# Sliding-window attention into a gated layer on one core: the first tile's first layer by halves of its weights, 96 tiny matmuls at the start, and some scores run twice

## The chip, the core and the metric

The kernel runs on one core of a Trainium2 chip. The metric is the device time of one execution in microseconds (us), as the median of several runs. Engines are written as in the profile: PE is TensorE's matmul, PEld its weight load, DVE is VectorE, ACT ScalarE, POOL GpSimd and SP SyncE.

## What is computed

Attention with a causal window of 64 positions over 8 batches, 8 heads, 576 positions and 64 values per head, then a gated layer on the 4608 rows that come out (512 wide, 1536 hidden):

```python
scores = scale * np.matmul(q, k.transpose(0, 1, 3, 2))
mask = (rel >= 0) & (rel < window)          # rel = query position - key position
attn = softmax(np.where(mask, scores, -1e9))
x = np.matmul(attn, v)                      # then heads side by side: (4608, 512)
gate = np.maximum(x @ w_gate, 0.0)
val = x @ w_val
out = (gate * val) @ w_out                  # float32
```

## The kernel before

The rows are cut into tiles: four of 384 rows (tiles 0 to 3) and six of 512. Attention is made in units of 192 rows, two for each of the first four tiles. A unit's scores are small matmuls in four row groups of 32 partitions (`st_block`, line 265), each block of 64 columns in two parts; `u_exp` (ACT) and `u_mask` (DVE) follow, `u_pv` multiplies with v (line 336), `u_recip`, `u_norm` and `u_turn` (DVE, and for half of unit 1 ACT in `u_norm_act`) divide and transpose the result into `xt`, the layer's input. For units 0 and 1 the mask is written into the score banks beforehand by matmuls of an identity with a bias tile (`bias_mm`, line 232, called by `u_bias`).

Tiles 0 and 1 use the plain layer, `hidden`: for a group of up to four blocks of 128 hidden columns it first runs the gate weights `wg` and then the value weights `wv` (line 589), each with four products that accumulate over the four 128-row chunks c of xt. ACT takes the gate result to SBUF (`relu`, line 572), DVE multiplies it with the value result out of PSUM into `g_sb` (`gate`, line 575). Results go to single PSUM banks 0 to 3 in turn (`one_bank`); units use banks 4 to 7 in pairs (`two_banks`). Tile 0's first group runs over two spans of 192 rows, unit 0's and then unit 1's; the other groups of tile 0 over all 384 rows. Tile 1 does its first 192 rows, then part of tile 0's output (`output`, line 1023), then its other rows. Tiles 2 and later use a scheme with seven products in place of eight (`fast_hidden`, line 634, and for the last six tiles also `SevenOut` and `SevenLast`, line 847), whose sums of weights DVE and POOL form on the way (`w_form`).

`w_load` brings four blocks of wg or wv by two transfers issued on POOL, one for chunks 0 and 1 and one for chunks 2 and 3. POOL also copies v rows (`v_spread`, line 215), loads q, k and v, and so its order of issue is written out by hand.

A planner (`Weaver`, `W`) writes the order in which instructions are emitted. It has a clock of its own, in which every matmul has a cost; `W.at(T, fn)` puts a piece of work in a heap for time T, and `W.advance` emits all that is due. `w_need` moves the clock to the time that `w_load` was told for the weights' landing. These times are no waits on the chip: they decide only the order on each engine. On the chip, engines wait for one another by semaphores on tiles and banks.

`keep_hot` and `heat` are matmuls on a cleared tile. The order of the products of each late tile is a list of names; for the last tile but one it is `SEVEN[-1]`, where P5a and P5b are two parts of product P5 and "v0", "v1" and "h1" are attention values and the beginning of the next tile's layer.

Of the kernel before, what the change touches and what calls it, by code (L numbers as in the profile page):

```python
# [47 lines left out]
def kernel(  # L48
# [20 lines left out]
    G = 4  # L69
# [84 lines left out]
    def w_load(wt, src, f0, f1, landed):  # L154

        if wt is not wo:
            ns = slice(128 * f0, 128 * f1)
            for a in range(2):
                nc.gpsimd.dma_start(wt[:, 2 * a:2 * a + 2, ns], src.rearrange("(a p e) n -> a p e n", a=2, e=2)[a, :, :, ns])  # L159
        if wt is wo:  # L160
            nc.gpsimd.dma_start(wo[:, f0:f1], src.rearrange("(c p) n -> p c n", p=128)[:, f0:f1])
        w_done.update(((wt.name, f), landed) for f in range(f0, f1))

    def w_need(wt, f):
        while (wt.name, f) not in w_done:
            W.pop()
        W.advance(w_done[wt.name, f])

# [51 lines left out]
        for g0, g1 in (((2, 3),), ((4, 5),), ((6, 9),))[uu]:  # L220
            rows(t[0:64, g0:g1:2], t[64:128, g0 - 1:g1 - 1:2])

    def heat(n, to, start=True):

        for _ in range(n):
            nc.tensor.matmul(to, zero[:, 0:128], zero[:, 0:to.shape[1]], start=start, stop=start, skip_group_check=not start)

    def keep_hot(to):
        nc.tensor.matmul(to, zero32[:, 0:128], zero32[:, 0:to.shape[1]], start=False, stop=False, skip_group_check=True)
# [31 lines left out]
    def st_block(to, g, hh, n, biased=False, later=False):  # L261

        b, w = divmod(n, NG)
        rows = slice(32 * g, 32 * g + 32)
        return [lambda dh=dh: nc.tensor.matmul(  # L265
            to, kTs[b % 2][rows, hh, 64 * w:64 * w + 128, dh], qTs[b % 2][rows, hh, 64 * w:64 * w + 64, dh],
            start=(dh == 0 and not biased and not later), stop=(dh == 1), skip_group_check=biased or later) for dh in range(2)]

    def run_rows(rows):

        for step in zip(*rows):
            for dh in range(2):
                for block in step:
                    block[dh]()
# [5 lines left out]
            bias_mm(units[u]["st"][c])  # L280
        units[u]["biased"] = True

    def u_st(u, hhs=(0, 1)):
        d = units.setdefault(u, {})
        if "st" not in d:
            st_tiles(u)
        run_rows([[st_block(d["st"][g][:, U * hh + 64 * w:U * hh + 64 * w + 64], g, hh, UB * u + w, "biased" in d)
                   for hh in hhs for w in range(UB)] for g in range(G)])
        return 0.29 * len(hhs)

    def p_of(u, h, w):
# [262 lines left out]
        while normed[0] < n:  # L554
            W.pop()

    def hidden(t, spans, f0=0, f1=NF, each=1):

        if t not in gs:
            gs[t] = g_sb_p.tile([128, NF, WT], FP16, name="g_sb"), {}  # L560
        g_sb, done = gs[t]
        xt = xt_tile(t)
        n = spans[0][1] - spans[0][0]

        w = 512 // n
        each = max(each, w)

        def part(tile):
            return tile[:, 0:w * n].rearrange("p (w n) -> p w n", w=w)

        def relu(r_sb, h1):
            nc.scalar.activation(part(r_sb), part(h1), ACT.Relu)  # L572

        def gate(f, c0, r_sb, h2):
            nc.vector.tensor_tensor(g_sb[:, f:f + w, c0:c0 + n], part(r_sb), part(h2), MUL)
            done.update(dict.fromkeys(range(f, f + w), c0 + n))

        for fb in range(f0, f1, each):
            r2s = [f_sb.tile([128, 2, WT], FP32, name="pr", bufs=4) for _ in range(2)]
            r_sbs = {}  # L580
            for i, wt in enumerate((wg, wv)):
                for c0, f in ((c0, f) for c0, _ in spans for f in range(fb, fb + each, w)):
                    h = one_bank()
                    part_written([h])
                    for b in range(w):
                        W.advance(W.clock)
                        w_need(wt, f + b)
                        for c in range(NC):
                            nc.tensor.matmul(h[:, b * n:b * n + n], wt[:, c, (f + b) * 128:(f + b) * 128 + 128],  # L589
                                             xt[:, c, c0:c0 + n], start=(c == 0), stop=(c == NC - 1))  # L590
                        W.clock += 4 * (n + 7) / 2400.0
                    if i == 0:
                        r_sb = r_sbs[c0, f] = r2s[len(r_sbs) // 2][:, len(r_sbs) % 2]
                        W.at(W.clock, lambda r_sb=r_sb, h=h: relu(r_sb, h))
                    else:
                        W.at(W.clock, lambda f=f, c0=c0, r_sb=r_sbs[c0, f], h=h: gate(f, c0, r_sb, h))

    def fast_hidden(t, seven=None):

# [467 lines left out]
    XAT = -0.3  # L1067
    SEVEN_LAST = (("P6", "P5", "P2", "P7", "oP1", "P3", "P4"), ("P6", "P5", "P2", "P7", "oP1", "P4", "P3"))
    SEVEN = {n: ("P2", "v0", "v1", "P6", "P5a", "P7", "s0", "P5b", "P4", "s1", "P3") for n in (-5, -4, -3, -2)}
    SEVEN[-1] = ("v0", "P2", "P6", "v1", "P5a", "P7", "P5b", "P4", "h1", "P3")  # L1070

    SEVEN[0] = ("P2", "P4", "P5", "P6", "P7", "P3")

    with tc.manual_schedule():
# [21 lines left out]
        k_zeros()  # L1096
        band_bias()

        first_round("k", (dve, act))
        u_bias(0)  # L1100
        u_bias(1)
# [21 lines left out]
        u_turn(0)  # L1123
        for hh in range(2):
            u_pv(1, (hh,), True)
        heat(1, units[1]["st"][3])
# [6 lines left out]
        w_load(*G3[1], 20.3)  # L1133
        w_load(*V3[1], 22.8)
        v_load(2)
        w_load(*G3[2], 27.0)
        w_load(*V3[2], 29.6)
        W.at(23.2, lambda: u_st(2))
        plan_exps(23.2, 2)
        plan_values(27.4, 2)  # L1140

        v_spread(2, pool)
        for name in "kq":
            for hh in range(2):
                qk_load(1, name, hh)
# [3 lines left out]
        for u in (4, 5):  # L1149
            v_load(u)  # L1150
        for i, (name, hh) in enumerate((n, hh) for n in "kq" for hh in range(2)):
            W.at(31.6 + 1.4 * i, lambda name=name, hh=hh: qk_trans(1, name, hh))
        for hh, T in enumerate((36.6, 38.8)):
            W.at(T, lambda hh=hh: u_st(3, (hh,)))
            for i in range(G):
                W.at(T + 0.4 + 0.22 * i, lambda hh=hh, i=i: u_exp(3, i, (hh,)))
                W.at(T + 0.8 + 0.22 * i, lambda hh=hh, i=i: u_mask(3, i, (hh,)))
            W.at(T + 3.5 - 0.7 * hh, lambda hh=hh: u_pv(3, (hh,)))
            W.at(T + 4.0 - 0.7 * hh, lambda hh=hh: u_recip(3, (hh,)))
            W.at(T + 4.1 - 0.7 * hh, lambda hh=hh: u_norm(3, hh))  # L1160
            W.at(T + 4.6 - 0.7 * hh, lambda hh=hh: u_turn(3, (hh,)))
        W.at(37.4, lambda: v_spread(3, pool))
        W.at(40.6, lambda: behind_masks(3))

        def pair(t, TA, TB, P):
            for u, T in ((2 * t, TA), (2 * t + 1, TB)):
# [10 lines left out]
            W.at(T + 1.9, lambda: u_turn(u))  # L1177
            return took

        plan_batch(2, (36.5, 36.6, 42.5, 42.6), (52.0, 53.6, 56.9, 57.1))  # L1180
        plan_batch(3, 58.0, None)
        W.at(58.0, lambda: v_load(8))
        for u in (6, 7):
# [1 line left out]
            W.at(58.0, lambda u=u: v_spread(u))  # L1185
        for u in (4, 5):
            W.at(45.6, lambda u=u: v_spread(u))
        pair(2, 46.6, 50.0, 54.0)
        W.at(52.7, lambda: behind_masks(5))
        pair(3, 62.6, 65.3, None)  # L1190
        W.at(68.0, lambda: behind_masks(7))
# [28 lines left out]
        def ahead(t):  # L1220
            T = W.clock
            long = widths[t] == WT
            ends = T + (32.7 if long else 22.5)
            if t + 2 <= LAST:
                qk_turns(t + 2, T, LATE if t - 1 in FAST_OUT else (0.1, 1.4, 8.0, 14.2) if long else (0.1, 1.4, 6.1, 10.7) if t < NS - 1 else (2.4, 6.1, 10.7, 14.2))
                v_ahead(t + 2, ends, ends + VAT if t in FAST_OUT else ends - 5.0 if long else T + 3.0 if t == 2 else ends + 1.5)
# [8 lines left out]
        for T, gap, eng, some in ((40.5, 0.1, nc.gpsimd, sums[0][:4] + sums[1][:3]), (52.8, 0.1, nc.gpsimd, sums[1][3:8]),  # L1235
                                  (48.2, 0.6, nc.vector, sums[0][4:8]), (68.1, 0.1, nc.gpsimd, sums[0][8:]),
                                  (64.5, 0.7, nc.vector, sums[1][8:])):
            for i, (w, j, n) in enumerate(some):
                W.at(T + gap * i, lambda eng=eng, w=w, j=j, n=n: w_form(eng, (wg, wv)[w], n, j))
# [21 lines left out]
        while any(id(one) in unread for one in singles[:4]):  # L1261
# [73 lines left out]
```

## Time and profile before

| what | value |
|---|---|
| time, median of 3 runs | 302.2 us (301.69 to 302.36) |
| the profiled execution's own time | 302.04 us |
| its span, from the first to the last instruction | 300.3 us |
| PE busy | 289.6 us, 96% |
| DVE, ACT, POOL busy | 251.7, 196.0, 201.7 us |
| granted TensorE clock | 1.0 |
| instructions on PE | 4643 matmuls and as many weight loads |

Times within the execution count from the span's start. A row of the timeline gives start, length, engine, line, operation, tiles, shape and count of instructions that follow one another, and in brackets how long the engine was idle before and what ended that. Matmuls are pipelined and their ends are modelled, so neighbouring rows overlap.

### The profile page before, as it was taken

What the parts mean: (1) busy time and instruction counts of PE and PEld (TensorE: products, weight loads), DVE (VectorE), ACT (ScalarE), POOL (GpSimd) and SP (SyncE); (2) the same over time, 40 slices, a digit from 0 to 9 for tenths busy, and PEclk for the clock granted to TensorE, in tenths of its full rate; (3) what the DMA queues carried; (4) which work ended last, traced back from release to release, by engine and by line L of the source; (5) the groups of instructions that cost most, each with busy time, mean ns of one, the idle gap of its engine ahead of it and who ended that gap; (6) DMA issues with size and microseconds to landing.
All of it is one profiled execution on the core that took longest, in us unless ns stands there. A gap on an engine that the chain in (4) does not pass through costs nothing.

```text
span 300.3 us, 11073 instructions
## 1 busy us (share of the span) xinstructions
PE 289.6 (96%) x4643; PEld 239.4 (80%) x4643; DVE 251.7 (84%) x517; ACT 196.0 (65%) x408; POOL 201.7 (67%) x241
## 2 busy tenths in 40 slices
PE   4899999999999999999999999999999999999994
PEld 2475877748957975888888888888888888888894
DVE  5947895997995999789999899989858985896584
ACT  3545336258848848885798579857985698538850
POOL 8767689868957893985957595759375617441750
PEclk9999999999999999999999999999999999999999
DMA  7999999979919636911399239922911210031013
GB/s 216 183 196 194 194 197 179 160 131 241 80 40 181 164 70 149 146 42 38 61 219 120 60 53 219 126 57 53 173 37 35 74 41 0 3 103 41 0 38 105
DMA packets 59506, 33.20 MB, mean 111 GB/s; under 512 B 39552, under 2 KB 53824, under 8 KB 59456
## 3 DMA queue, kind: packets, MB, share of 16 engines
q0 software_dynamic: 46688, 18.29, 52.3%
q1 hardware_dynamic: 12192, 13.75, 15.1%
q8 instruction: 36, 0.59, 0.8%
q10 hardware_dynamic: 576, 0.46, 0.5%
q14 instruction: 14, 0.11, 0.1%
HBM read 37.75 MB, written 9.44 MB: 157 GB/s over the span
## 4 chain that ended last, share of the span: by engine, by line
PE 87%; DMA 5%; POOL 4%; DVE 2%; issue 1%; DVEq 0%; POOLq 0%
PE bank L634 46%; PE bank L847 17%; PE bank L589 7%; PE bank L767 5%; PE bank L1023 5%; PE bank L265 3%; DMA wg<-in_moe_w_gate_dram 3%; PE bank L465 2%; DMA v<-in_v_dram 2%; POOL v L205 1%; PE bank L336 1%; POOL wg L159 1%; DVE g_sb L659 1%; DVE g_sb L797 0%; POOL wv L159 0%
## 5 line engine op out<-in xcount | busy, mean ns | idle before, releaser
L659 POOL TENSOR_TENSOR g_sb<-pr 128x512 f16<-128x512 f32 (+1 forms) x36 | 42.7, 1193 | 43.6 <-ACT pr L676 43.6
L670 DVE TENSOR_TENSOR pr<-bank,pr 128x512 f32<-128x512 f32 (+1 forms) x96 | 58.5, 649 | 3.6 <-PE bank L634 1.9
L653 ACT COPY pr<-bank 128x512 f32<-128x512 f32 (+1 forms) x96 | 49.1, 566 | 13.7 <-PE bank L634 13.5
L659 DVE TENSOR_TENSOR g_sb<-r,bank 128x512 f16<-128x512 f32 (+1 forms) x48 | 31.3, 652 | 23.8 <-ACT r L703 22.4
L847 PEld LDWEIGHTS <-g_sb 128*128 128x128 f16 x444 | 41.8, 98 | 5.2 <-issue 0.2
L634 PE MATMUL bank<-xc,vs 128*128 128x256 f16 (+1 forms) x288 | 41.3, 266 | 0.0
L634 PE MATMUL bank<-xc,us 128*128 128x256 f16 (+1 forms) x288 | 41.3, 266 | 0.0
L634 PEld LDWEIGHTS <-vs 128*128 128x128 f16 x384 | 36.5, 98 | 3.5
L634 PEld LDWEIGHTS <-us 128*128 128x128 f16 x384 | 36.5, 98 | 3.3
L205 POOL DMA_DIRECT2D v<-in_v_dram x41 | 34.7, 866 | 2.2 <-DMA nats<-in_q_dram 1.0
L676 ACT ACTIVATE pr<-pr 128x512 f32<-128x512 f32 (+1 forms) x48 | 29.3, 610 | 9.8 <-DVE pr L670 9.8
L703 ACT ACTIVATE r<-bank 128x512 f32<-128x512 f32 (+1 forms) x48 | 27.7, 577 | 4.8 <-PE bank L634 4.0
L634 PEld LDWEIGHTS <-wg 128*128 128x128 f16 x288 | 27.4, 98 | 3.2
L634 PEld LDWEIGHTS <-wv 128*128 128x128 f16 x288 | 27.4, 98 | 2.6
L634 PE MATMUL bank<-xt,wg 128*128 128x256 f16 (+1 forms) x192 | 27.5, 266 | 0.0
L634 PE MATMUL bank<-xt,wv 128*128 128x256 f16 (+1 forms) x192 | 27.5, 266 | 0.0
L797 POOL TENSOR_TENSOR g_sb<-g_sb,xus 128x512 f16<-128x512 f16 x24 | 27.1, 1148 | 0.0
L847 PE MATMUL bank<-wo,g_sb 128*128 128x256 f16 (+1 forms) x222 | 26.6, 270 | 0.0
L430 ACT ACTIVATE pw<-bank 128x512 f16<-128x512 f32 x48 | 25.3, 605 | 1.1 <-PE bank L265 0.7
L847 PE MATMUL bank<-wts,g_sb 128*128 128x256 f16 (+1 forms) x222 | 25.4, 270 | 0.2 <-DVE xw L484 0.2
L643 ACT COPY bank<-bank 128x512 f32<-128x512 f32 (+1 forms) x48 | 24.6, 553 | 0.0
L572 ACT ACTIVATE pr<-bank 128x384 f32<-128x384 f32 x24 | 11.9, 501 | 15.5 <-PE bank L589 12.5
(107 smaller groups left out, 559.8 us busy)
## 6 DMA issues: line engine op xcount, KB each, us to landing
out_dram<-o_sb SPq DMA_DIRECT2D x30, 256.0 KB, 3.1
nats<-in_k_dram POOLq DMA_DIRECT2D x15, 288.0 KB, 6.1
nats<-in_q_dram POOLq DMA_DIRECT2D x15, 288.0 KB, 8.0
v<-in_v_dram POOLq DMA_DIRECT2D x31, 128.0 KB, 8.2
v<-v SPq DMA_DIRECT2D x27, 66.0 KB, 2.7
v<-v SPq DMA_DIRECT2D x13, 132.0 KB, 2.5
wg<-in_moe_w_gate_dram POOLq DMA_DIRECT2D x6, 256.0 KB, 6.4
wv<-in_moe_w_val_dram POOLq DMA_DIRECT2D x6, 256.0 KB, 8.1
```

The source lines that it names most:

```text
L205: nc.gpsimd.dma_start(v16s[b % 2][lo:hi, g, :, 0:64], v[b, :, 64 * g - 64 + lo:64 * g - 64 + hi].rearrange("h p d -> p h d"))
L430: nc.scalar.activation(d["p"][g].rearrange("p n c -> p (n c)"), d["st"][g], ACT.Exp, scale=scale)
L589: nc.tensor.matmul(h[:, b * n:b * n + n], wt[:, c, (f + b) * 128:(f + b) * 128 + 128], xt[:, c, c0:c0 + n], start=(c == 0), stop=(c == NC ...
L634: nc.tensor.matmul(to[:, HT * m:HT * m + HT], w[:, k, 128 * m:128 * m + 128], x[:, k], start=(first and m == 0 and k == 0), stop=(k == 1), ...
L643: nc.scalar.copy(at[j, "B", i][:, 0:TW], at[j, "A", i][:, 0:TW])
L653: nc.scalar.copy(pr[:, i], at[j, "A", i][:, 0:TW])
L659: eng.tensor_tensor(gh[:, f:f + 2, h], pair(r), pair(v), MUL)
L670: nc.vector.tensor_tensor(pr[:, i], to[:, 0:TW], pr[:, i], ADD)
L676: nc.scalar.activation(pr[:, 0], pr[:, 0], ACT.Relu)
L703: nc.scalar.activation(r, to[:, 0:TW], ACT.Relu)
L797: eng.tensor_tensor(to, x, y, op)
L847: nc.tensor.matmul(at[key][:, QN * m * whole:QN * m * whole + n1 - n0], A[:, 128 * m:128 * m + 128], B[:, c, n0:n1], start=(first and m == ...
```

## The change

Four things change, and times of the planner with them.

1. `hidden` gets `halves`. With it a group's blocks are first all run over chunks 0 and 1 and then all over chunks 2 and 3, so that the first half needs only the first of the two transfers; each block has its own bank for the time of both halves. For tile 0's first group the gate weights are still done span by span, the value weights for both spans together. It is used for all of tile 0. `w_load` and `w_need` keep a landing time for each half.
2. `hidden` also gets `banks`. Tile 1's first rows use the banks 0, 1, 4, 5, 2, 3, 0, 1, 2, 3, 0, 1 in place of 0 to 3 in turn, and tile 0's output is done in one piece of three blocks, before the rest of tile 1's first layer.
3. `heat` can multiply any cleared tile. 96 matmuls with two weight columns and two moving columns, on the first cleared tile (`warm`), go ahead of the bias matmuls.
4. `u_st(2, again=4)` runs the first four score blocks of each row group of unit 2 twice, with the same result.

Beside these, times of unit 3, of batch transposes, of units 4 and 5 and of some loads move, and in `SEVEN[-1]` P5 is no longer cut and goes behind P7.

```diff
-        w_done.update(((wt.name, f), landed) for f in range(f0, f1))
+        w_done.update(((wt.name, f, a), landed - 1.3 * (1 - a)) for f in range(f0, f1) for a in range(2))
...
-    def heat(n, to, start=True):
+    def heat(n, to, by):
 
         for _ in range(n):
-            nc.tensor.matmul(to, zero[:, 0:128], zero[:, 0:to.shape[1]], start=start, stop=start, skip_group_check=not start)
+            nc.tensor.matmul(to, by[:, 0:to.shape[0]], by[:, 0:to.shape[1]], start=True, stop=True)
...
-    def u_st(u, hhs=(0, 1)):
+    def u_st(u, hhs=(0, 1), again=0):
...
+        run_rows([(2 * row)[:again] + row for row in rows])
...
-    def hidden(t, spans, f0=0, f1=NF, each=1):
+    def hidden(t, spans, f0=0, f1=NF, each=1, halves=False, banks=None):
...
+                items = [[(c0, f) for f in range(fb, fb + each, w)] for c0, _ in spans]
+                if halves and i == 1:
+                    items = [sum(items, [])]
+                for group in items if halves else [[item] for items_ in items for item in items_]:
+                    hs = [singles[banks.pop(0)] if banks else one_bank() for _ in group]
+                    part_written(hs)
+                    for cs in ((0, 1), (2, 3)) if halves else (range(NC),):
+                        for (c0, f), h in zip(group, hs):
+                            for b in range(w):
+                                W.advance(W.clock)
+                                w_need(wt, f + b, cs[-1] // 2)
+                                for c in cs:
+                                    nc.tensor.matmul(h[:, b * n:b * n + n], wt[:, c, (f + b) * 128:(f + b) * 128 + 128],
+                                                     xt[:, c, c0:c0 + n], start=(c == 0 and not (halves and b)), stop=(c == NC - 1),
+                                                     skip_group_check=halves)
...
-    SEVEN[-1] = ("v0", "P2", "P6", "v1", "P5a", "P7", "P5b", "P4", "h1", "P3")
+    SEVEN[-1] = ("v0", "P2", "P6", "v1", "P7", "P5", "P4", "h1", "P3")
...
+        heat(96, units[0]["st"][0][0:2, 0:2], warm[:, 0:1].bitcast(FP16))
...
-        W.at(23.2, lambda: u_st(2))
+        v_spread(2, pool)
+        W.at(23.2, lambda: u_st(2, again=4))
         plan_exps(23.2, 2)
-        plan_values(27.4, 2)
-
-        v_spread(2, pool)
+        plan_values(27.6, 2)
...
-            W.at(31.6 + 1.4 * i, lambda name=name, hh=hh: qk_trans(1, name, hh))
-        for hh, T in enumerate((36.6, 38.8)):
+            W.at((32.0, 33.4, 34.8, 36.2)[i], lambda name=name, hh=hh: qk_trans(1, name, hh))
+        for hh, T in enumerate((37.6, 39.8)):
...
-        pair(2, 46.6, 50.0, 54.0)
+        pair(2, 46.6, 50.0, 55.7)
...
-        hidden(0, ((0, U), (U, TT)), 0, 4, 4)
-        hidden(0, ((0, TT),), 4, NF, 4)
-        hidden(1, ((0, U),), each=4)
-        output(0, (0, 1), (0, 8, NF))
+        hidden(0, ((0, U), (U, TT)), 0, 4, 4, True)
+        hidden(0, ((0, TT),), 4, NF, 4, True)
+        hidden(1, ((0, U),), each=4, banks=[0, 1, 4, 5, 2, 3, 0, 1, 2, 3, 0, 1])
+        taken["one"] += 2
+        output(0, (0, 1, 2), (0, 4, 8, NF))
         ready(1)
         hidden(1, ((U, TT),), each=4)
-        output(0, (2,))
```

More of the change, by code (lines that the diff above doesn't have):

```diff
@@ L161, in w_load, with w_need @@
             nc.gpsimd.dma_start(wo[:, f0:f1], src.rearrange("(c p) n -> p c n", p=128)[:, f0:f1])
-        w_done.update(((wt.name, f), landed) for f in range(f0, f1))
-    def w_need(wt, f):
-        while (wt.name, f) not in w_done:
+        w_done.update(((wt.name, f, a), landed - 1.3 * (1 - a)) for f in range(f0, f1) for a in range(2))
+    def w_need(wt, f, a=1):
+        while (wt.name, f, a) not in w_done:
             W.pop()
-        W.advance(w_done[wt.name, f])
+        W.advance(w_done[wt.name, f, a])
     nat = {}
@@ L286, in u_st @@
             st_tiles(u)
-        run_rows([[st_block(d["st"][g][:, U * hh + 64 * w:U * hh + 64 * w + 64], g, hh, UB * u + w, "biased" in d)
-                   for hh in hhs for w in range(UB)] for g in range(G)])
+        rows = [[st_block(d["st"][g][:, U * hh + 64 * w:U * hh + 64 * w + 64], g, hh, UB * u + w, "biased" in d)
+                 for hh in hhs for w in range(UB)] for g in range(G)]
+        run_rows([(2 * row)[:again] + row for row in rows])
         return 0.29 * len(hhs)
@@ L581, in hidden @@
             for i, wt in enumerate((wg, wv)):
[L582 to L596, printed above, removed]
+                items = [[(c0, f) for f in range(fb, fb + each, w)] for c0, _ in spans]
@@ new lines, in hidden @@
+                if halves and i == 1:
[12 more added lines that the diff above has]
+                                                     skip_group_check=halves)
+                                W.clock += len(cs) * (n + 7) / 2400.0
+                            if cs[-1] < NC - 1:
+                                continue
+                            if i == 0:
+                                r_sb = r_sbs[c0, f] = r2s[len(r_sbs) // 2][:, len(r_sbs) % 2]
+                                W.at(W.clock, lambda r_sb=r_sb, h=h: relu(r_sb, h))
+                            else:
+                                W.at(W.clock, lambda f=f, c0=c0, r_sb=r_sbs[c0, f], h=h: gate(f, c0, r_sb, h))
@@ L1125 @@
             u_pv(1, (hh,), True)
-        heat(1, units[1]["st"][3])
+        heat(1, units[1]["st"][3], zero)
         for hh in range(2):
@@ L1132 @@
             u_turn(1, (hh,))
-        w_load(*G3[1], 20.3)
-        w_load(*V3[1], 22.8)
+        w_load(*G3[1], 21.6)
+        w_load(*V3[1], 24.1)
         v_load(2)
@@ L1157 @@
                 W.at(T + 0.8 + 0.22 * i, lambda hh=hh, i=i: u_mask(3, i, (hh,)))
[L1158 to L1161, printed above, removed]
+            W.at(T + 3.5, lambda hh=hh: u_pv(3, (hh,)))
+            W.at(T + 4.0, lambda hh=hh: u_recip(3, (hh,)))
+            W.at(T + 4.1, lambda hh=hh: u_norm(3, hh))
+            W.at(T + 4.6, lambda hh=hh: u_turn(3, (hh,)))
         W.at(37.4, lambda: v_spread(3, pool))
-        W.at(40.6, lambda: behind_masks(3))
+        W.at(41.6, lambda: behind_masks(3))
         def pair(t, TA, TB, P):
@@ L1178, in unit_values @@
             return took
-        plan_batch(2, (36.5, 36.6, 42.5, 42.6), (52.0, 53.6, 56.9, 57.1))
+        plan_batch(2, (36.5, 36.6, 42.5, 42.6), (52.0, 52.9, 56.9, 57.1))
         plan_batch(3, 58.0, None)
@@ L1225, in ahead @@
                 qk_turns(t + 2, T, LATE if t - 1 in FAST_OUT else (0.1, 1.4, 8.0, 14.2) if long else (0.1, 1.4, 6.1, 10.7) if t < NS - 1 else (2.4, 6.1, 10.7, 14.2))
-                v_ahead(t + 2, ends, ends + VAT if t in FAST_OUT else ends - 5.0 if long else T + 3.0 if t == 2 else ends + 1.5)
+                v_ahead(t + 2, ends, ends + VAT if t in FAST_OUT else ends - 5.0 if long else T + 6.5 if t == 2 else ends + 1.5)
                 if t + 1 == NS:
@@ L1234 @@
         sums = {w: [(w, j, n) for j in range(NF // 4) for n in (0, 1, 3, 2)] for w in (0, 1)}
-        for T, gap, eng, some in ((40.5, 0.1, nc.gpsimd, sums[0][:4] + sums[1][:3]), (52.8, 0.1, nc.gpsimd, sums[1][3:8]),
+        for T, gap, eng, some in ((41.5, 0.1, nc.gpsimd, sums[0][:4] + sums[1][:3]), (52.8, 0.1, nc.gpsimd, sums[1][3:8]),
                                   (48.2, 0.6, nc.vector, sums[0][4:8]), (68.1, 0.1, nc.gpsimd, sums[0][8:]),
```

## The prediction

> **What bounds the kernel now.** I read the page, then the chain of waits, then TensorE's (PE's) timeline with its idle column, then VectorE's (DVE's) rows inside the stretch that this pointed to.
>
> The page's first section says which engine the whole span hangs on:
>
> ```profile
> PE 289.6 (96%) x4643; PEld 239.4 (80%) x4643; DVE 251.7 (84%) x517; ACT 196.0 (65%) x408; POOL 201.7 (67%) x241
> ```
>
> PE is busy for 96% of 300.3 us, so only its idle places can be won. The chain that ended last shows where the start hands over to PE:
>
> ```profile
> 17.34 0.66 POOL wg L159
> 18.00 9.04 DMA wg<-in_moe_w_gate_dram
> 27.05 0.04 issue
> 27.09 0.50 PE bank L589 x2
> ```
>
> Up to 27.1 us the chain is transfers, after it almost only PE. PE's timeline from there to 295 us names one wait (0.18 us at 263.59, below). Before it, the first layer of tile 0 looks so (start, length, form, count, idle before and what ended it):
>
> ```profile
> 13.84 0.33 PE L589 MATMUL bank<-xt,wg 128*128 128x192 f16 x2
> 14.51 1.33 PE L589 MATMUL bank<-xt,wg 128*128 128x192 f16 x14 [0.35 <-DMA wg<-in_moe_w_gate_dram]
> 16.50 1.48 PE L589 MATMUL bank<-xt,wg 128*128 128x192 f16 x16 [0.66 <-DVE xt L379]
> 17.82 2.80 PE L589 MATMUL bank<-xt,wv 128*128 128x192 f16 x32
> 20.45 2.76 PE L589 MATMUL bank<-xt,wg 128*128 128x384 f16 x16
> 23.15 0.55 PE L265 MATMUL bank<-qT,kT 32*128 32x64 f16 x48
> 23.63 2.77 PE L589 MATMUL bank<-xt,wv 128*128 128x384 f16 x16
> 26.24 0.49 PE L589 MATMUL bank<-xt,wg 128*128 128x384 f16 x2
> 27.09 0.50 PE L589 MATMUL bank<-xt,wg 128*128 128x384 f16 x2 [0.36 <-DMA wg<-in_moe_w_gate_dram]
> 27.52 0.56 PE L336 MATMUL bank<-v,p 128*32 128x65 f16 x48
> 28.01 2.12 PE L589 MATMUL bank<-xt,wg 128*128 128x384 f16 x12
> 29.97 2.76 PE L589 MATMUL bank<-xt,wv 128*128 128x384 f16 x16
> ```
>
> Ends are modelled, so I use starts. From 17.82 to 20.45 go 32 matmuls: 0.0825 us each at 192 columns. From 23.63 to 26.24 go 16: 0.163 us each at 384. So the three stalls, start to start, are 14.51 - 13.84 - 2 x 0.083 = 0.50 us, 16.50 - 14.51 - 14 x 0.083 = 0.83, and 27.09 - 26.24 - 2 x 0.163 = 0.52: 1.85 us, all that halves can attack.
>
> **The change part by part.** The terms are PE's time at each stage, after against before.
>
> *First span, gate weights.* The eight matmuls on the first half of the weights run from 13.84 to 14.50, in the time that was a wait; the second half lands (14.5, from the wg tile's rows: issue 8.13, 6.3 to landing) as they end. The span is done at 15.17, not 15.68: 0.5 gained, but the second span can't start at once.
>
> *Second span.* Its first half needs only the first transposed half of xt. DVE's rows end that at 15.53 and the other at 16.38. So 8 matmuls run from 15.6 to 16.25 and the rest from 16.43-16.50: done at 17.14 against 17.82. Gain 0.68. It is bounded by 0, because before, PE started only at 16.50 though its first two operands were there at 15.53; I take 0.68, since the code's wait is for the half alone.
>
> *Value weights 0 to 3.* Landed at 16.4 and 17.5, no wait. 32 matmuls: PE is free at 17.14 + 2.64 = 19.78.
>
> *What halves cost.* Now the four banks of a group finish 0.33 us apart, where before each took 0.65, and each must be read by DVE before the next group may write it. DVE can't keep that pace:
>
> ```profile
> 18.75 2.54 DVE L575 TENSOR_TENSOR g_sb<-pr,bank 128x384 f16<-128x384 f32 x4 [2.36 <-PE bank L589]
> ...
> 27.20 1.00 DVE L575 TENSOR_TENSOR g_sb<-pr,bank 128x384 f16<-128x384 f32 x2
> ```
>
> Two gates back to back take 1.00 us, one 0.54: 0.46 us apart. A gate starts 0.27 after its item's last matmul is issued (17.82 + 8 x 0.0825 = 18.48 to 18.75). In the new order the value group's first item ends at 17.14 + 1.65 = 18.79, its gate at 19.61, the others at 20.07, 20.53 and 20.99. PE reaches the banks at 19.78, 20.11, 20.43 and 20.76 and waits for the last until 21.05 (0.05 from release to start, as with xt: 13.79 to 13.84). Loss 0.3. The gate group then ends at 21.05 + 0.33 + 1.30 = 22.68 against 20.45 + 2.61 = 23.06: gain left, 0.38.
>
> *Scores run twice.* 4 blocks x 4 row groups x 2 = 32 more matmuls; the 48 of before cost 23.63 - 23.06 = 0.57 with the switch, or 0.0075 to 0.010 each by the rows of 48. So 0.24 to 0.32 on PE with nothing beside it; I take 0.28. Gain left 0.10. Value weights 4 to 7 (landed 22.4 and 23.2) don't hold PE: it starts at 23.53 and ends at 26.14.
>
> *The third gate group.* Its first half landed at 25.8, so that 8 matmuls can run before the half that lands at 27.05: the 0.52 stall goes. What is late next is DVE again: first gate from 25.15 + 0.27 = 25.42 to 25.97, a mask of unit 2 behind it (two masks take 0.61, so 0.27 apart), then gates ending at 26.70, 27.16 and 27.62. PE, there at 26.14, gets its fourth bank at 27.67 instead of 27.12: loss 0.55. Then 0.33, the 48 matmuls on v (28.01 - 27.42 = 0.59) and 8 x 0.163: done at 29.89, against 29.97. Net of all so far, 0.08.
>
> *After it.* Value weights 8 to 11 (28.4 and 29.6) come in time. ScalarE's relus (0.49, 0.38 apart) keep up. Layer one of tile 1 writes banks 4 and 5 for its first value items, so that the last four gates hold nobody. The other new times move queued work by 0.4 to 1.7 us: the query transposes end at 36.56 now and 37.6 by DVE's order then, and PE asks for them at 38.1 instead of 36.66, as four score matmul groups now stand behind more of layer one. The output's three blocks need wo rows that land at 39.5, 42.0 and 44.6, and PE reaches them at about 41, 44 and 46. Value loads moved 3.5 us later serve work some 30 us on. All that at nothing, hidden behind PE's own rows; if one cover is gone it costs a wait of a few tenths. `v_spread(2, pool)` moves only past lines that queue work for later, past no issue on POOL or SP.
>
> *The last tile but one.* P7 goes ahead of all of P5:
>
> ```profile
> 262.82 0.59 ACT L883 COPY o_sb<-bank 128x512 f32<-128x512 f32 x1 [0.71 <-PE bank L847]
> 263.59 4.09 PE L847 MATMUL bank<-wts,g_sb 128*128 128x256 f16 x36 [0.18 <-DVE xw L484]
> ```
>
> P5 waited for a bank; P7 waits for the ACT copy that ends at 263.41, so PE starts at 263.46. Gain 0.13. P4's copy then hides behind 12 matmuls (1.31) instead of 8.
>
> *The 96 tiny matmuls.* They can start at about 1.0 (the memset ends at 0.95) and PE's first work now is at 4.41. No row shows one. From below: the 64-column ones, 0.0075 each. From above: a bias matmul at the start, (6.92 - 4.41) / 8 = 0.31. They all fall on one column group; the v matmuls take 0.010 in four, hence 0.04 in one, the nearest row: 96 x 0.04 = 3.8, to 4.8. Then bias (2.5 at most) and the two 384-column passes (1.4) end by 8.7 if all stay as slow as now, and by 7 at the speed that the same form has at 9.16 (0.91 for two, not 1.42). DVE's qT lets the scores start at 8.38. So I take nothing; the point is below.
>
> The bias rows (0.31 for 384 columns, against 0.163 later) show PE at half its later speed at the start. [...]
>
> **The sum.** -0.08 at 29.9, -0.13 at 263: 302.04 of the profiled execution (span 300.3 and 1.7 around it) becomes 301.83. That execution lies 0.16 below the median of 302.2, within its runs (301.69 to 302.36). I forecast 301.8 us: by some 0.1% less, inside the 0.2% that a measurement here can tell.
>
> **Rivals.** *The banks hold less than I say.* If gates released each bank in time, the losses of 0.30 and 0.55 vanish, and 301.8 becomes 301.0. Against: the 0.46 us between gates. For: a release could come earlier than a gate's recorded end, and runs whose weights land later than in this profile cost the kernel before more than the new one, which has 1.5 us in hand at 27.05.
> *The second span waits for both halves, as it seems to do now.* 0.68 gone: 302.5.
> *The tiny matmuls are in the way, slower than before.* The two passes must end by 8.34. With the bias at full speed (1.3) and passes of 0.9 the tiny ones may end at 6.1, 0.053 each; with both slow at 4.4, 0.035. My 0.04 lies between. At 0.07 they end at 7.7; scores, exponentials and xt come 1.6 later, less ACT's idle of 0.27 at 10.94: 303.1. For it: cold rows at half speed; against: only two columns are loaded and streamed.
> *Instructions run out.* The third section has 36 fetches of 16 KB for PE:
>
> ```profile
> q8 instruction: 36, 0.59, 0.8%
> ```
>
> 16.4 KB over 256 instructions is a block; 192 more at the front shift every border, and a burst of 200 in a microsecond could meet one unfetched: about 1 us late, 302.9. Against: no idle on PE after 27.1 but one, with 33 blocks fetched there. [...]
>
> **How the numbers follow.** Forecast 0.42 (its own range 301.3 to 302.4: faster by over 0.2% in 0.13, within in 0.26, slower 0.03). Banks hold less: 0.22, faster. Both halves: 0.14, half within 0.2% and half slower. Tiny ones: 0.14, slower. Instructions: 0.08, slower. Faster 0.35, same 0.33, slower 0.32. From 301.0 to 303.1 lie 8 in 10.
>
> **What would show it.** Right: eight matmuls before 14.51; L589 rows at 15.6; idle on PE ended by DVE g_sb L575 ahead of the second and third gate groups, 0.3 and 0.5; the last value group of tile 0 starting at 29.9; P7 at 263.46. Wrong: scores later than 8.4 (tiny ones), the second span still at 16.5, no bank waits, or a new wait on PE past 30 us.

## The result and the profile after

The changed kernel takes 302.98 us (median of 7 runs, 302.61 to 303.68) against 301.95 us of the kernel before on the same chip (7 runs): a ratio of 1.0035, interval 1.0023 to 1.0047. It is slower by 1.0 us, where I forecast 301.8. Its profiled execution took 303.32 us, with a span of 301.6. Of some variants below, the other runs were slower than the profiled one, at lower granted clocks (e2: 305.3 to 306.7 us at 0.989 to 0.999, against 303.76 us in the profile), for a reason that is open, so causes are read from the traces.

The page's first section after, engines with busy time and instructions:

```profile
PE 293.1 (97%) x4771; PEld 241.8 (80%) x4771; DVE 251.6 (83%) x517; ACT 195.4 (65%) x408; POOL 201.1 (67%) x241
```

PE has 128 matmuls more (96 tiny, 32 doubled scores) and is busy for a larger share: it waits less and yet ends later. PE's timeline after, from the start to the third group of layer one (line 589 is now 595, 336 is 337, 379 is 380):

```profile
1.00 2.54 PE L226 MATMUL bank<-warm 128*2 128x2 f16 x96 [1.00 <-DVE warm L1092]
4.40 2.72 PE L232 MATMUL bank<-bias,ident 128*128 128x384 f16 x8 [0.86 <-DVE bias L129]
...
9.06 0.55 PE L265 MATMUL bank<-qT,kT 32*128 32x64 f16 x48 [0.66 <-DVE qT L199]
...
11.46 0.55 PE L265 MATMUL bank<-qT,kT 32*128 32x64 f16 x48 [0.70 <-DVE qT L199]
...
15.45 1.48 PE L595 MATMUL bank<-xt,wg 128*128 128x192 f16 x16
17.20 1.67 PE L595 MATMUL bank<-xt,wg 128*128 128x192 f16 x16 [0.27 <-DVE xt L380]
18.70 2.80 PE L595 MATMUL bank<-xt,wv 128*128 128x192 f16 x32
21.34 3.07 PE L595 MATMUL bank<-xt,wg 128*128 128x384 f16 x16
24.34 0.82 PE L265 MATMUL bank<-qT,kT 32*128 32x64 f16 x80
25.09 2.77 PE L595 MATMUL bank<-xt,wv 128*128 128x384 f16 x16
27.70 1.98 PE L595 MATMUL bank<-xt,wg 128*128 128x384 f16 x8
...
31.41 2.76 PE L595 MATMUL bank<-xt,wv 128*128 128x384 f16 x16
```

Start against start, after minus before: the first span +1.61 (15.45 and 13.84), value weights +0.88 (18.70 and 17.82), second gate group +0.89, the scores behind it +1.19 (so 0.30 for banks), the value group behind them +1.46 (0.27 for the doubled scores), the third gate group +1.46, the last value group +1.44 (31.41 and 29.97: the wait of 0.52 us for weights is gone and waits for banks of the same size stand there). The difference is still +1.43 where tile 2 starts (70.51 and 69.08), and +1.21 at 295 us. Everything was lost by 31 us. My sum had -0.08 us there, so it missed by 1.52; where the value weights start it had -0.68, and 0.88 was measured, a miss of 1.56. The failure lies ahead of that point: the first half of xt that the second span needs is ready at 17.14 us, before it was at 15.53.

Scores now run at 9.06 and 11.46 us, before at 8.38 and 10.54. Ahead of them the loads land later: k at 5.24 us (4.69 before), q at 6.65 (6.13), the second half of k at 8.86 (7.56), the last v at 12.70 (11.61). The chain of waits up to the second span runs through one of these loads, which lands at 11.88 us, before at 10.66:

```profile
5.00 6.88 DMA v<-in_v_dram
...
13.58 0.24 PE bank L337 x8
...
16.57 0.59 DVE xt L380
...
17.20 0.82 PE bank L595 x8
```

Queue q8, which the page calls instruction, I take to bring PE's instructions: with 128 matmuls and 128 weight loads more, and the instructions of DVE, ACT and POOL as many as before, the page's third section counts one transfer of 16 KB more (36 before):

```profile
q8 instruction: 37, 0.61, 0.8%
```

The first of these transfers (a fetch, below) starts at 6.72 us, among those loads, where before it started at 14.15; it takes 0.96 us.

### The profile page after: what moved, and what is told of

Same layout as the page of the kernel before. It is cut to its first block, busy times and chain, and to the rows that moved or that the text cites. A ratio compares the mean times of both kernels' runs of the same rounds, so it can differ in the third digit from the quotient of the medians.

```text
span 301.6 us, 11333 instructions
## 1 busy us (share of the span) xinstructions
PE 293.1 (97%) x4771; PEld 241.8 (80%) x4771; DVE 251.6 (83%) x517; ACT 195.4 (65%) x408; POOL 201.1 (67%) x241
## 4 chain that ended last, share of the span: by engine, by line
PE 92%; DMA 2%; DVE 2%; POOL 1%; issue 0%; ACT 0%; DVEq 0%; POOLq 0%
PE bank L643 46%; PE bank L856 18%; PE bank L595 10%; PE bank L776 5%; PE bank L1032 5%; PE bank L265 4%; PE bank L466 2%; DMA v<-in_v_dram 2%; PE bank L337 1%; DVE v L215 0%; POOL nats L179 0%; DVE xt L380 0%; DVE g_sb L576 0%; POOL v L205 0%; PE bank L229 0%
## 5 line engine op out<-in xcount | busy, mean ns | idle before, releaser
L300 ACT ACTIVATE p<-bank 128x192 f16<-128x192 f32 (+1 forms) x44 | 14.3, 418 | 12.2 <-PE bank L265 12.1
```

## The experiments

### First runs: what the tiny matmuls and the doubled scores do

Theory A: the extra instructions move the first fetch from 14.1 to 6.7 us, in among the loads. Theory B: the tiny matmuls cost nothing, and the loss is waits for banks and doubled scores. Theory C: PE's early activity itself does harm.

```diff
 e1_no_tiny (from the changed kernel)
-        heat(96, units[0]["st"][0][0:2, 0:2], warm[:, 0:1].bitcast(FP16))
 e2_tiny_alone (from the kernel before)
+        heat(96, units[0]["st"][0][0:2, 0:2], warm[:, 0:1].bitcast(FP16))
 e3_six_long (from the changed kernel)
-        heat(96, ...)
+        for _ in range(6): nc.tensor.matmul(<2 x 512 of the same bank>, warm, <warm, 512 columns>, start=True, stop=True)
 e4_no_again (from the changed kernel)
-        W.at(23.2, lambda: u_st(2, again=4))
+        W.at(23.2, lambda: u_st(2))
```

> The changed kernel without the 96 tiny matmuls. Theory A (their 192 PE instructions bring the first fetch of a 16 KB instruction block from 14.1 to 6.7 us, among the loads of k, q and v, and layer one starts late): the first fetch is back after 12 us, the first layer-one matmul at 13.8 instead of 15.45, and the time falls by 0.7 to 1.2 us, to about the time of before (301.8 to 302.3). Theory B (the tiny matmuls cost nothing; the first loads were late by chance in that one profile, and the loss is in the bank waits and the doubled scores): the time stays within 0.3 us of the changed kernel's.

> The kernel before with the 96 tiny matmuls alone. Theory A: first fetch near 6.7 us, layer one's first matmul 1.0 to 1.6 us later than 13.84, time 0.7 to 1.2 us over before. Theory B: within 0.2 us of before.

> The changed kernel with 6 matmuls of 512 columns on the same zeros in place of the 96 tiny ones: PE is as busy from 1.0 to 3.5 us, but with 12 instructions in place of 192. Theory A (the count of instructions): as without them, 0.7 to 1.2 us under the changed kernel, first fetch after 12 us. Theory C (PE's early activity, through the clock or the memory ports, is what harms): as slow as the changed kernel. Theory B: no difference from it either, but then the run without them shows none as well.

> The changed kernel with unit 2's scores run once. By the sum: 32 matmuls of 0.0082 to 0.010 us less, and all behind them is bound by the chain of gates, so the time falls by 0.25 to 0.33 us. If the extra matmuls filled a wait for weights, no change; if they moved an instruction fetch out of the way, slower.

Measured: 302.89, 305.78, 303.59 and 304.25 us, ratios 1.003 (1.0019 to 1.0041), 1.012 (1.0095 to 1.0144), 1.0056 (1.0043 to 1.0069) and 1.0083 (1.0064 to 1.0102). Theory A has the start right: without tiny matmuls (e1), or with six long ones (e3), the first fetch is at 14.36 and 14.12 us and layer one begins at 13.83 and 13.82; with the tiny ones alone (e2) they are at 6.24 and 15.11. Theory C falls with e3, where PE is busy as long and k lands at 4.67 us. But the times do not follow: without the tiny matmuls nothing is won, as theory B had it for e1. And e4, without the doubled scores, which cost 0.27 us, is slower still: its fastest run, 303.71 us, lies above the changed kernel's slowest, 303.68. For e4 I had named that case: slower, if the repeats moved a fetch out of the way.

The timelines say why. Without tiny matmuls the first span runs through without a stall, as forecast. Then the second span waits longer than ever, though DVE had ended the two halves of its tokens (its rows of xt) at 15.53 and 16.37 us:

```profile
13.83 1.48 PE L595 MATMUL bank<-xt,wg 128*128 128x192 f16 x16
16.77 1.48 PE L595 MATMUL bank<-xt,wg 128*128 128x192 f16 x16 [1.46 <-DVE xt L380]
```

And with six long matmuls in place of the tiny ones, the stall sits in the middle of the first span, whose operands were all there (the last, half of the weights, since 14.25 us). The idle column finds nothing that ended it ("issue"), there and in a second place:

```profile
13.82 0.98 PE L595 MATMUL bank<-xt,wg 128*128 128x192 f16 x10
16.50 1.98 PE L595 MATMUL bank<-xt,wg 128*128 128x192 f16 x22 [1.69 <-issue]
...
63.15 2.33 PE L1032 MATMUL bank<-wo,g_sb 128*128 128x512 f16 x10 [0.53 <-issue]
```

Six matmuls were added, and the stall came six matmuls earlier in the kernel's order and ended at the same 16.50. So I counted. Before: 8 bias turns, 2 rows of keep_hot, 48 scores, 2, 48, 48 of v, 2, 48, 1, and 2 + 14 of layer one are 223 matmuls ahead of the one that starts at 16.50. With six more ahead, 10 of layer one ran: 223 again. Without tiny matmuls: 223. The stall's place is a number, not an operation. One transfer more had come with 128 matmuls and their weight loads, and before, 2 x 4643 instructions came with 36 transfers, 258 each; so I estimated a block of 256 instructions, 128 matmuls long, and 223 = 95 + 128: I took it for a border between two blocks. The later stalls with "issue" (0.9 us in e4, 1.08 in e2, 0.70 in e3) fit that: all sit at matmul 991 = 223 + 6 x 128, which is at another place in each kernel, after 72 and 80 of a row of 96 matmuls on v in e4 and e2 and among output matmuls in e3:

```profile
58.17 0.82 PE L337 MATMUL bank<-v,p 128*32 128x65 f16 x72
59.75 0.37 PE L337 MATMUL bank<-v,p 128*32 128x65 f16 x24 [0.75 <-issue]
```

(e4.) The doubled scores are 32 matmuls, so in the changed kernel matmul 991 comes after 40 of this row, not 72. Its block's transfer then begins at 53.19 us, in e4 only at 57.52, and there is no stall; why it is asked for so much earlier is not shown. That is theory D, which the next runs test: PE runs out of instructions where 128 matmuls pass sooner than a block can be fetched. Most borders of the traces pass without a stall, in the changed kernel all of them; at these it is 0.3 to 3.0 us.

### Second runs: other numbers, and the waits for banks

```diff
 f1_88_tiny, f2_128_once (from the changed kernel; in f2 also u_st(2) in place of u_st(2, again=4))
-        heat(96, ...)
+        heat(88, ...)        # f2: 128
 f3_groups_whole (from e1)
-        hidden(0, ((0, TT),), 4, NF, 4, True)
+        hidden(0, ((0, TT),), 4, NF, 4)
 f4_88_pairs (from f1)
+                if halves and n == TT:
+                    items = [g[k:k + 2] for g in items for k in (0, 2)]
```

> The changed kernel with 88 tiny matmuls in place of 96. Theory D (instruction blocks): TensorE's instructions arrive in blocks of 16 KB, 128 matmuls with their weight loads, with borders at matmul 95, 223, 351 and so on, counted from 0; passing a border asks for the block after next, whose transfer begins about 3.2 us later and which can run 2.35 us after that. With 96 tiny matmuls border 95 is passed at 3.5 us and the transfer falls among the k and q loads; with 88 it is the last bias matmul, so the transfer should begin between 7.6 and 9.9 us, k lands at 4.7 us as without tiny matmuls, the first scores run at 8.4 us, layer one begins at 13.9 to 14.6 us (15.45 with 96), its second span at 15.6 to 16.4 us (17.20 with 96), and the median is 301.8 to 302.4 us. Theory E (the tiny matmuls' own activity disturbs the loads, whatever their number): as with 96, 302.7 to 303.1 us.

> The changed kernel with 128 tiny matmuls and the score blocks run once: all later borders lie where they lie in the changed kernel, since 32 matmuls were added ahead of what the doubled scores took away. Theory D: the stall of 0.9 us at matmul 991 that showed when the scores ran once with 96 tiny matmuls is gone; the start is as late as in the changed kernel (layer one at 15.3 to 15.6 us), and the time is the changed kernel's less the 0.27 us of the repeats, 302.5 to 303.0 us. Theory F (the repeated scores help by themselves, by their place or by keeping TensorE's clock up): as with the scores run once before, 303.9 to 304.5 us.

> The changed kernel without tiny matmuls, and with halves in the first group of layer one alone (the second and third group run whole, as before the change). Theory D: the second span cannot start before about 16.5 to 16.8 us (matmul 223 is its first), so the halves gain nothing there; with no halves behind it the waits for banks (0.31 and 0.52 us) are gone, and the doubled scores lie in the wait for the third group's weights (27.0 us), so the time is that of before within 0.3 us: 301.7 to 302.2 us, with a short stall at matmul 1375 left. Theory G (the halves' waits for banks cost nothing, since the time is lost elsewhere): 302.7 to 303.1 us, as without tiny matmuls.

> The changed kernel with 88 tiny matmuls, and the second and third group's banks taken by halves two at a time in place of four. Theory D: start as with 88 tiny matmuls alone, and the waits for banks of 0.31 and 0.52 us mostly gone (0.0 to 0.3 us left), since a bank's second half follows its first half by two matmul groups and the gates' banks come free one after another: 0.3 to 0.8 us below the run with 88 alone, 301.2 to 301.9 us. Theory G (the waits for banks hide waits for weights that come instead): the same as with 88 alone within 0.15 us.

Measured: 304.08 (1.0087, 1.0063 to 1.0112), 303.52 (1.0052, 1.0038 to 1.0067), 303.92 (1.0067, 1.0054 to 1.0081) and 303.63 us (1.0056, 1.0042 to 1.007). All four medians missed what theory D led me to expect; the stalls sit where it says: at matmul 991 in f1, 351 in f2, 223 and 1375 in f3, and at no border in f4.

With 88 the first fetch still started at 6.41 us and k landed at 5.25: it is asked for earlier than at matmul 95. With 128 and scores once, the stall at matmul 991 is gone, as theory D says and theory F does not, and a new one has come at matmul 351 = 223 + 128, again the second span's first:

```profile
14.93 1.48 PE L595 MATMUL bank<-xt,wg 128*128 128x192 f16 x16
17.63 1.48 PE L595 MATMUL bank<-xt,wg 128*128 128x192 f16 x16 [1.21 <-DVE xt L380]
```

With whole groups (f3) the second and third group run without a wait for banks: from 18.59 to 30.48 it takes 11.89 us, without tiny matmuls and with halves 12.82 (18.09 to 30.91). So those waits are real. But what was won went again: gates came late at 56.33 and 61.65 (0.67 and 0.76 us of idle, ended by the gate line), since the planner's times were made for another schedule, and a border at matmul 1375 = 223 + 9 x 128 cost 0.7 us (its fetch had begun 2.35 us before PE went on, while the idle column names ACT). In f4 the pairs took 9.27 us from the second gate group to the third value group (21.05 to 30.32) and fours with 88 tiny matmuls 10.16 (20.43 to 30.59), and again late gates at 55.70 and 57.25 gave it back.

### Third runs: the border further back, and the parts alone

```diff
 g1_62_tiny (from the changed kernel), g2_before_62 (the kernel before with this line alone)
+        heat(62, ...)
 g3_before_half_pairs (from the kernel before: hidden, w_load and w_need of the change, pairs as in f4)
+        hidden(0, ((0, U), (U, TT)), 0, 4, 4, True)
+        hidden(0, ((0, TT),), 4, NF, 4, True)
 g3 and g4_p7_alone (from the kernel before)
-    SEVEN[-1] = ("v0", "P2", "P6", "v1", "P5a", "P7", "P5b", "P4", "h1", "P3")
+    SEVEN[-1] = ("v0", "P2", "P6", "v1", "P7", "P5", "P4", "h1", "P3")
```

> The changed kernel with 62 tiny matmuls. Over ten traces the first block of instructions begins its transfer 3.4 to 3.8 us after matmul 63 to 80 has run, so 88 were still too many: matmul 80 ran at 3.2 us. With 62, matmuls 63 to 71 are bias matmuls and run from 4.4 to 6.9 us. Theory D (the block's transfer disturbs the loads): it begins between 7.8 and 10.6 us, k lands at 4.7 us, the first scores run at 8.4 us, layer one begins at 13.9 to 14.6 us, and its second span at 15.6 to 16.5 us without a wait for instructions; all later borders lie 34 matmuls later in the kernel's order than in the changed kernel, about as with the scores run once, so a stall of 0.5 to 1.0 us at matmul 991 is expected: 302.2 to 303.0 us in all. Theory E (the tiny matmuls disturb the loads by themselves): k lands at 5.1 to 5.3 us as with 88, 96 and 128.

> The kernel before with 62 tiny matmuls and nothing else. Theory D: no wait at the second span for instructions any more (it starts at 15.9 to 16.3 us in place of 16.50, once its first span's weights are there), and the second half of the third group's weights at 27.0 us still sets the end of the start, so no more than 0.2 us is gained by 30 us; later borders are moved, and one or two stalls of 0.3 to 1.0 us may come (a stall only where matmul number 223 plus a multiple of 128 is reached): 301.8 to 303.2 us. Theory E: as with 96 tiny matmuls alone in the kernel before, layer one at 15.1 us.

> The kernel before with layer one's first tile by halves (the second and third group's banks two at a time) and P7 ahead of P5 in the tile of SEVEN[-1], and nothing else: no tiny matmuls, scores once, all planned times as before. Theory D: the number of TensorE instructions is that of before, so every border lies where it did; the second span still waits for instructions until 16.5 us, the third group's wait of 0.52 us for weights shrinks to 0 to 0.3 us, and P7 ahead of P5 gives 0.13 us: 301.3 to 301.8 us. Theory G (halves bring waits for banks of their own size): 301.8 to 302.3 us.

> The kernel before with P7 ahead of P5 in SEVEN[-1] alone. All theories: 0.13 us less, 301.7 to 301.95 us, seen as a gap less at 263 us in the trace.

Measured: 304.86 (1.0103, 1.0086 to 1.012), 304.77 (1.0098, 1.0074 to 1.0121), 301.84 (1.0004, 0.9995 to 1.0013) and 301.47 us (0.9993, 0.9984 to 1.0001), with 301.72 before.

With 62 the fetch starts at 13.03 and 12.86 us, not between 7.8 and 10.6: what asks for it comes, I estimate from these starts, later than matmul 71, and by the run with 88 before matmul 88. My expectation of a start without a stall was wrong for that reason. In both kernels matmul 223 (62 + 8 + 2 + 48 + 2 + 48 + 48 + 2 + 3) stalls, until 15.24; here the kernel before with 62:

```profile
13.79 0.21 PE L336 MATMUL bank<-v,p 128*32 128x65 f16 x3
15.24 0.82 PE L336 MATMUL bank<-v,p 128*32 128x65 f16 x45 [1.24 <-issue]
```

Both stall at 991 too (0.72 and 0.85 us). And k lands at 5.02 and 5.04 us, late although no fetch is near: the tiny matmuls delay the first load by themselves (theory E), the fetch adds to it at the second half of k (8.45 to 8.94 us where it falls there, 7.83 and 7.96 here, 7.41 to 7.62 without tiny matmuls).

The third kernel (halves with pairs, and P7) leaves all borders where they were. Its second span starts at 16.76, its third group waits for neither weights nor banks, its trace is 0.24 us early at 42 us and loses 0.19 of it by 59 us: no gain. So its time is theory G's, but not for the reason that G gives. P7 ahead of P5 alone is the best of all, by 0.25 us where I expected 0.13; its interval just reaches 1. Part of that is luck: in its trace the third group's weights land at 26.63 us, not 27.05, and the last value group starts at 29.55, not 29.97, long before the place of this edit.

### Fourth and fifth runs: few tiny matmuls, and fewer matmuls

```diff
 h1_24_tiny, h2_44_tiny (from the changed kernel)
-        heat(96, ...)
+        heat(24, ...)        # h2: 44
 i1_24_fewer (from e1), i2_half_24_fewer (from g3): unit 1's P by V as half as many matmuls of 64 columns
-                    for j in range(G):
+                    for j in range(0, G, 2 if u == 1 else 1):
...
```

> The changed kernel with 24 tiny matmuls. Theory E in its first form (any tiny matmuls delay the first load): k lands at 5.0 us or later, as with 62, 88, 96 and 128 (5.02 to 5.25 us in eight traces). Theory H (it takes a number of instructions: TensorE's stream of instructions asks for something more once some fixed matmul between 24 and 62 is reached): k lands at 4.5 to 4.85 us as in the six traces without tiny matmuls. Both: the stalls at matmuls 223 and 991 stay where they are in number; matmul 223 is now a matmul of the second P by V product, stops at about 13.4 us and goes on 2.3 to 2.4 us after the first transfer of instructions begins (12.5 to 14.5 us).

> The changed kernel with 44 tiny matmuls: the same question with the number between. Theory E: k lands at 5.0 us or later. Theory H: below or above that according to where the fixed matmul lies. Both: a stall at matmul 223, which ends 2.3 to 2.4 us after the first transfer of instructions begins.

> The changed kernel without tiny matmuls, and with 24 matmuls fewer ahead of layer one: the second unit's P by V products run as 24 matmuls of 64 columns in place of 48 of 32, which leaves half of that unit's attention values wrong and takes 0.2 to 0.3 us of matmuls out. Theory D (the second span waits for instructions): matmul 223, which was the second span's first, is now a matmul of wv's first group, due at about 17 us when its instructions have long come (16.4 to 16.8 us); so the second span starts when its tokens are turned, 15.4 to 15.9 us, in place of 16.77 us, and 30 us is reached 0.6 to 1.3 us earlier than without tiny matmuls. Every later border moves by 24 too, so stalls further on may come or go (0 to 0.9 us). Theory X (the second span waits for its tokens, as the profile's column says): it starts at 16.5 to 16.8 us as before.

> The kernel before with layer one by halves (banks two at a time), P7 ahead of P5, and the same 24 matmuls fewer, with half of the second unit's values wrong. Theory D: its second span starts at 15.4 to 15.9 us in place of 16.76, wv at 16.8 to 17.2 us, the third group still waits a little for the second half of its weights (26.2 to 27.0 us), and layer one's first tile is over 0.4 to 1.0 us earlier than with halves and all 48 matmuls (32.32 us there). Theory X: second span at 16.5 us or later, nothing gained.

With 24 and 44, 306.72 us (1.0163, 1.0086 to 1.0239) and 305.08 (1.0108, 1.0072 to 1.0145), in two runs each. Matmul 223 stalls in both, by 0.31 us from the start before it with 44 and by 3.00 with 24; both stall at 991 again (1.55 and 0.90).

With 24:

```profile
13.71 0.51 PE L337 MATMUL bank<-v,p 128*32 128x65 f16 x41
17.02 0.24 PE L337 MATMUL bank<-v,p 128*32 128x65 f16 x7 [2.81 <-issue]
```

The fetch began at 14.74, 2.28 us before. That is 3.6 us after matmul 84, as elsewhere, but 4.6 after matmul 83: by that estimate what asks for it lies no earlier than at 84. k landed at 4.90 with 24 and 5.27 with 44, against 4.50 to 4.85 in eight traces without tiny matmuls: 24 lie between the two expectations, so what in the tiny matmuls delays it stays open.

The last two take 24 matmuls away and leave half of unit 1's attention values wrong. i1 took 302.48 us (1.0035, 1.0012 to 1.0058), i2 305.07 (1.0129, 1.0074 to 1.0184). The second span of i1:

```profile
13.81 1.48 PE L596 MATMUL bank<-xt,wg 128*128 128x192 f16 x16
15.55 1.67 PE L596 MATMUL bank<-xt,wg 128*128 128x192 f16 x16 [0.26 <-DVE xt L381]
17.06 2.80 PE L596 MATMUL bank<-xt,wv 128*128 128x192 f16 x32
```

It starts at 15.55, 1.22 us earlier than without tiny matmuls, and in i2 at 15.54. Now the wait is one for tokens, and the tokens had been no later without tiny matmuls: the first half of xt ends at 15.49 us here and at 15.53 there. That settles it: until 16.77 PE had waited for its instructions, whose fetch began at 14.36. All traces say the same. They have 21 stalls at such borders, and PE always went on 2.2 to 2.4 us after that border's own fetch had begun (the first fetch belongs to matmul 223, the next to 351 and so on), whatever the idle column names.

In the kernel before the border hid behind the tokens, because the old order needs the second half of xt, ended at 16.38, for the third matmul of the span. e2, with its borders elsewhere, runs two matmuls and then waits for xt. So I estimate that the border cost the kernel before 0.2 us: 14 matmuls from 16.43 would have ended at 17.59, and ended at 17.82.

But i2, a full 1.02 us ahead at the first tile's end (31.30 and 32.32), gave it all back at another border, matmul 863 = 223 + 5 x 128:

```profile
54.37 1.04 PE L337 MATMUL bank<-v,p 128*32 128x65 f16 x64
56.68 0.42 PE L337 MATMUL bank<-v,p 128*32 128x65 f16 x32 [1.27 <-issue]
```

and at 143 us once more (0.81 us, at matmul 2270, which is one ahead of 223 + 16 x 128, so that this one is not shown to be a border).

## Why the prediction was wrong, step by step

Two steps failed. The measured kernel pays for the first loads, which the tiny matmuls delay; without tiny matmuls the second span's gain would have failed by itself.

- **First span: right.** Its 16 matmuls run without a stall wherever the halves are and no border falls among them, as it does in e3 (16 in one row at 13.83 without tiny matmuls, at 15.45 with them).
- **Second span, gain 0.68: wrong, the first of two steps that failed.** I took the start at 15.6 because the code's wait is for the first half alone. That is so (15.55 in i1; 0.06 us behind that half in the changed kernel). But before, PE stood until 16.50 although its first operands were there at 15.53, and I had seen that; I wrote the lower bound of 0 down and then followed the idle column, which named xt. There was a second wait, for the instruction block of matmul 223. Without tiny matmuls it ends at 16.77, and nothing is gained.
- **The tiny matmuls, cost nothing: right on PE, wrong for the loads. This is the step that the measured kernel pays for.** They take 0.025 us each from start to start (I took 0.04), end at 3.54 and move neither bias nor passes (4.40 and 6.91 us, before 4.41 and 6.92). They do move the border away from the second span, so that in the changed kernel it waits for tokens alone (0.27 of idle). But with them k lands 0.55 us later and the first fetch falls among the loads, the last v lands 1.09 later, and xt for the second span is ready 1.61 later: all of the 1.56 missed where the value weights start. My reason for nothing was that qT ends last, at the time it had before; that the loads ahead of qT would stay where they were I took for granted. e1 and e2 show the cause, as the delay goes and comes with this one line; its size varies, with layer one starting at 14.54 to 15.56 in the six traces with 88 or more. How much is the first load's delay and how much the fetch among the loads is open. Either way the second span begins 0.3 to 0.7 us later than before: 16.77 without, 17.20 with.
- **The bias turns: no faster behind the tiny matmuls.** The 1.3 us that my rival gives them at full speed is in no run: their row has 2.72 us for eight with the tiny matmuls as without; only six matmuls of 512 columns in the same time (e3) made it 1.60. The profile's granted clock reads 1.00 in all three, so only the rows tell, and why is not shown. It is worth nothing either way: in e3, with 1.60, the scores start at 8.36 us, after a wait of 1.72 for qT, against 8.38 before.
- **Waits for banks: right in the changed kernel, in part by luck.** Forecast 0.30 and 0.55, read 0.30 and 0.52. But the 0.55 was worked out for a start that the changed kernel does not have. In i1, which has it, the second wait is 1.0 us, so that term was about half of what it should have been. With f3 the waits vanish, with f4 mostly.
- **Doubled scores: right in size** (forecast 0.28, read 0.27) **and wrong in sense.** "With nothing beside it" left out that 32 matmuls move every later border; without them matmul 991 costs 0.9 us.
- **The third group's weights, and the rest to 70 us: right.** The changed kernel is no test of the weights, as it reaches them at 27.70 when all had landed by 26.96; but i2 starts that group at 25.50 and does not wait, though the second half lands at 26.07. The difference of +1.44 at 31.41 is +1.43 at 70.51, so nothing that moved shows as late.
- **P7 ahead of P5: right.** The difference to before falls from 1.34 to 1.21 us across it, and the wait that stood at 263.59 before is gone (after: at 264.80, no idle).
- **The sum.** With both failed steps out of the way (i1), the last value group starts at 30.27 against my 29.89: of the 1.52 missed there 0.38 stay, by the banks, which then hold PE for 1.0 us ahead of the third group. So the forecast was too low even with them. By the whole time less is known: i1's trace ends 0.06 us behind the trace of the kernel before, but its median of 302.48 lies 0.78 above the 301.70 measured beside it, and that difference is open.
- **The rivals.** "Instructions run out", at 0.08, was the mechanism that takes the second span's gain without tiny matmuls, and that costs several variants time. It is not what the changed kernel itself pays: there each fetch begins at least 2.7 us before its border is reached, and none stalls. I priced what 192 more instructions would do and held against it that PE had no idle after 27 us, and never asked whether the stalls before 27 us were of that kind already. "Tiny matmuls in the way" came true by the loads, not by PE's time; that its 303.1 is so near 302.98 is luck, since its 1.6 us were to come from tiny matmuls of 0.07 us.

## What to carry to other kernels

Before you price the end of a wait, check that the releaser named in the idle column came when the engine started; where both halves of xt were there 0.4 us earlier, as without tiny matmuls, something else held the engine (16.77 against 16.37 us in e1). Count the instructions: if stalls of several variants sit at one number modulo 128 matmuls, and a transfer on the instruction queue began 2.2 to 2.4 us before PE went on, I read it as PE waiting for its instruction blocks; earlier data won nothing there (e1: first half of xt at 15.53 us, start at 16.77). Price work added at the start by what it does to the loads, too, and not only by its engine's time (k landed 0.55 us later here). Edits that added or took PE instructions moved the place of later borders (e3 by 6 matmuls, i1 by 24), and their time was their own cost plus whatever the borders then met, 0.3 to 3.0 us a stall; judge it by the trace's stalls, not by the total alone.

## What the runs showed of the hardware

PE's stalls fell at matmul 223 in the kernel before and in nine variants, and at 223 plus 128, 5 x 128, 6 x 128 or 9 x 128 in others: 21 stalls of 0.3 to 3.0 us, each of which ended 2.2 to 2.4 us after that border's fetch began. In all eighteen traces the first fetch began 3.1 to 3.9 us after matmul 87 had started. Where matmul 223 stalled, 5.8 to 6.1 us had passed since matmul 87; where 7.0 or more had passed, it did not stall. Later in the changed kernel the same stretch of 136 matmuls, further on by a multiple of 128, passed in as little as 2.43 us without a stall. Fetches there began up to 1.7 us before the matmul in the place of 87, so the count alone does not forecast a stall.

From start to start a matmul of two by two columns takes 25 ns, and a doubled score of 64 columns in four row groups 8 ns (0.27 us for 32). With 44 or more tiny matmuls ahead of everything, k lands at 5.02 to 5.27 us (nine traces), and without at 4.50 to 4.85 (eight, the one with six long matmuls at 4.67); why is open.
